# Moving the Winograd transforms of a residual block to float16 tiles and merged operations, and rescheduling its group-norm statistics

## The chip, the cores and the metric

The kernel runs on one core of one Trainium2 chip. The metric is the device time of one execution in microseconds (us), the median over the runs that are quoted. The kernel before takes 567.0 us in six runs.

The engines are named as in the profile: PE (TensorE matmuls), PEld (TensorE weight loads), DVE (VectorE), ACT (ScalarE), POOL (GpSimd) and SP (SyncE, which issues most DMAs). A line such as L628 is a line of the kernel file.

## The reference

The function is one residual block of a diffusion network, with B = 2 samples, C = 512 channels, 64 x 64 pixels and an embedding of E = 1152, all in bfloat16.

```python
def reference(x, t_emb, g1, be1, w1, w_emb, g2, be2, w2):
    def gn(z, gamma, beta): ...        # group norm, 4 groups, eps 1e-5
    def conv3(z, w): ...               # 3x3 convolution, padding 1, 512 -> 512 channels
    h = conv3(silu(gn(x, g1, be1)), w1)
    h = h + (silu(t_emb) @ w_emb).reshape(B, C, 1, 1)
    h = conv3(silu(gn(h, g2, be2)), w2)
    return x + h
```

## The kernel before

Each convolution is a Winograd transform F(4,3) along the rows: four output rows are made from six "positions" of six input rows. The work is cut into 32 **sets**. A set is one layer (of 2), one chunk of 32 image rows (4 chunks: two samples of two chunks) and one tile of 128 output channels (`ot`, 4 of them). A set has 6 positions x 4 input channel tiles (`ct`) x 3 column taps = 72 matmuls of 128x128 weights on 128x512 data, so the 32 sets have 2304. I number the sets 1 to 32. Sets 1 to 16 are the first convolution (`layer == 0`), sets 17 to 32 the second.

Four kinds of work surround the matmuls:

- **U**, the transformed weights. For each of the 32 pairs (`ot`, `ct`) of the two layers, TensorE transposes nine 128x128 blocks into PSUM, ScalarE copies them out and VectorE forms the four mixed positions.
- **V**, the transformed input of a chunk. ScalarE applies group norm and SiLU to one channel tile, VectorE forms six positions from it. A chunk has four such parts, and the first set of a chunk (sets 5, 9, 13 ...) can't finish before all four are there.
- **The output transform** (`evac`): six PSUM banks of a set become four output rows.
- **Group-norm statistics.** Those of the second layer (`gn2`) end in a tiny matmul whose result stands in one of two shared PSUM banks (`ps_x`). The weight transposes of U go through the same two banks.

All but the matmuls is cut into steps that a small scheduler, `_Background`, hands out after each position of a set, earliest deadline first. A deadline is a slot number; a set has six slots.

The parts that the change touches (cuts marked with `...`):

```python
KAPPA = 1.0 / 6.0
...
def gn2_task(b, stats):                    # four output tiles, one step each
    for ot in range(CT):
        gn2_finalize(b, ot, *stats[ot])    # sums -> tiny matmul into ps_x -> scale and bias
        yield
...
def prep_U(layer, ot, ct, eng=None, dep=None):
    ...                                    # DMA of the weights, 9 transposes into pa, pb (ps_x)
    nc.scalar.copy(out=U[:, :, 0:NPOS:NPOS - 1, :], in_=pa[:])
    nc.scalar.copy(out=g1t[:], in_=pb[:])
    yield                                                    # sb_, U, g1t are BF16, cc is F32
    nc.vector.tensor_tensor(out=sb_[:], in0=g0, in1=g2, op=ALU.add)
    nc.vector.tensor_tensor(out=U[:, :, 1, :], in0=sb_[:], in1=g1t[:], op=ALU.add)
    nc.vector.tensor_tensor(out=U[:, :, 2, :], in0=sb_[:], in1=g1t[:], op=ALU.subtract)
    yield
    nc.vector.scalar_tensor_tensor(out=cc[:], in0=g0, scalar=0.25, in1=g2, op0=ALU.mult, op1=ALU.add)
    nc.vector.scalar_tensor_tensor(out=U[:, :, 3, :], in0=g1t[:], scalar=0.5, in1=cc[:], ...)
    nc.vector.scalar_tensor_tensor(out=U[:, :, 4, :], in0=g1t[:], scalar=-0.5, in1=cc[:], ...)
    yield
...
def produce_V(...):                        # one part; all tiles BF16
    nc.scalar.activation(out=at[...], in_=ap, func=ACT.Silu, bias=..., scale=...)
    yield
    nc.vector.tensor_scalar(out=vqf, in0=rows2(1), scalar1=4.0, ...)     # first chunk: on ScalarE
    nc.vector.tensor_tensor(out=vqf, in0=vqf, in1=rows2(3), op=ALU.subtract)
    nc.vector.tensor_tensor(out=Vc[:, 1], in0=p_, in1=q, op=ALU.add)
    nc.vector.tensor_tensor(out=Vc[:, 2], in0=p_, in1=q, op=ALU.subtract)
    nc.vector.tensor_tensor(out=vsf, in0=rows2(3), in1=rows2(1), op=ALU.subtract)
    nc.vector.tensor_scalar(out=s2, in0=s_, scalar1=2.0, ...)            # first chunk: on ScalarE
    nc.vector.tensor_tensor(out=Vc[:, 3], in0=r_, in1=s2, op=ALU.add)
    ...                                    # seven more: 5 tensor_tensor and 2 tensor_scalar of 528 columns
...
def evac(pos):                             # all temporaries F32
    if pos == 1:   nc.scalar.activation(out=c1[:], in_=accs[1][:], func=ACT.Copy, scale=KAPPA)
    elif pos == 2: # t1 = KAPPA*acc2 + c1 ; c1 = 2*c1 - t1           (2 scalar_tensor_tensor)
    elif pos == 3: nc.scalar.activation(out=c3[:], in_=accs[3][:], func=ACT.Copy, scale=KAPPA)
    elif pos == 4: # t2 = KAPPA*acc4 + c3 ; c3 = 2*c3 - t2 ; rows 1 and 2, tt, ss
                   # layer 0: 6 operations; layer 1: 10, with the residual rows
    elif pos == 0: # row 0 = acc0 + tt
    elif pos == 5: # row 3 = acc5 + ss, then the output DMA
...
for layer in range(2):
    for idx, (b, ch) in enumerate(chunks):
        for ot in range(CT):
            ...                            # one set: 6 x (12 matmuls, one scheduler tick, evac)
        if layer == 0 and ch == NCH - 1:   # sums of a sample complete: statistics of layer 2
            bg.finish(t_emb_task)
            t_gn2[b] = bg.add(gn2_task(b, ...), CT, slot_of(0, idx, CT - 1) + SLOTS + 2 * SLOTS)
```

Of the kernel before, what the change touches and what calls it, by code (L numbers as in the profile page):

```python
# [10 lines left out]
ALU = mybir.AluOpType  # L11
AX = mybir.AxisListType
F32 = mybir.dt.float32
BF16 = mybir.dt.bfloat16
PSUM = bass.MemoryType.PSUM
# [48 lines left out]
def kernel(  # L64
# [22 lines left out]
    NKX = 3  # L87
# [8 lines left out]
    KAPPA = 1.0 / 6.0  # L96
    FAST_U = "s"
    ACT_TS0 = True
    N_SUM_ACT = 1
    RES_ON_PE = False  # L100
# [20 lines left out]
    h_scr = dpool.tile([B, CT, P, HW], BF16, name="h_scr")  # L121
# [13 lines left out]
    a_tmp = [consts.tile([P, CR + 4, WP], BF16, name=f"a_tmp{i}") for i in range(2)]  # L135
    for at in a_tmp:
        nc.gpsimd.memset(at[:, :, 0:WP:WP - 1], 0.0)
    vq = consts.tile([P, TR, 2, WP], BF16, name="vq")
    vs = consts.tile([P, TR, 2, WP], BF16, name="vs")
    vq2 = consts.tile([P, TR, 2, WP], BF16, name="vq2")  # L140
    vt = consts.tile([P, 2, 3, TR, WP], BF16, name="vt")
# [119 lines left out]
    def gn2_finalize(b, ot, ssum, ssq):  # L261
        m0 = small.tile([P, 2], F32, name="m0")
        nc.vector.reduce_sum(out=m0[:, 0:1], in_=ssum[:], axis=AX.X)
# [24 lines left out]
    def prep_U(layer, ot, ct, eng=None, dep=None):  # L288
        wn = stage.tile([P, CQ], BF16, tag="stage")
        after((eng or nc.sync).dma_start(out=wn[:], in_=w_v[layer][ot][:, ct * CQ:(ct + 1) * CQ]),  # L290
              dep() if dep else None)
        U = upool.tile([P, NKX, NPOS, P], BF16, tag="U")
        Ut[layer][ot][ct] = U
        wn_v = wn[:].rearrange("p (c ky kx) -> p kx ky c", ky=3, kx=3)
        yield
        pa = ps_x.tile([P, NKX, 2, P], BF16, tag="x")
        for kx in range(NKX):
            for j in range(2):
                nc.tensor.transpose(pa[:, kx, j, :], wn_v[:, kx, 2 * j, :], ident[:])  # L299
        pb = ps_x.tile([P, NKX, P], BF16, tag="x")  # L300
        for kx in range(NKX):
            nc.tensor.transpose(pb[:, kx, :], wn_v[:, kx, 1, :], ident[:])
        nc.scalar.copy(out=U[:, :, 0:NPOS:NPOS - 1, :], in_=pa[:])  # L303
        g1t = wtmp.tile([P, NKX, P], BF16, tag="g1t")
        nc.scalar.copy(out=g1t[:], in_=pb[:])  # L305
        g0 = U[:, :, 0, :]
        g2 = U[:, :, NPOS - 1, :]
        if FAST_U == "both":
            g0q = wtmp.tile([P, NKX, P], BF16, tag="g0q")
            nc.scalar.activation(out=g0q[:], in_=pa[:, :, 0, :], func=ACT.Copy, scale=0.25)  # L310
            g1h = wtmp.tile([P, NKX, P], BF16, tag="g1h")
            nc.scalar.activation(out=g1h[:], in_=pb[:], func=ACT.Copy, scale=0.5)
            yield
            sb_ = wtmp.tile([P, NKX, P], BF16, tag="sb")
            nc.vector.tensor_tensor(out=sb_[:], in0=g0, in1=g2, op=ALU.add)
            nc.vector.tensor_tensor(out=U[:, :, 1, :], in0=sb_[:], in1=g1t[:], op=ALU.add)
            nc.vector.tensor_tensor(out=U[:, :, 2, :], in0=sb_[:], in1=g1t[:], op=ALU.subtract)
            yield
            cb_ = wtmp.tile([P, NKX, P], BF16, tag="sb")
            nc.vector.tensor_tensor(out=cb_[:], in0=g0q[:], in1=g2, op=ALU.add)  # L320
            nc.vector.tensor_tensor(out=U[:, :, 3, :], in0=cb_[:], in1=g1h[:], op=ALU.add)
            nc.vector.tensor_tensor(out=U[:, :, 4, :], in0=cb_[:], in1=g1h[:], op=ALU.subtract)
            yield
            return
        if FAST_U == "s":
            yield
            sb_ = wtmp.tile([P, NKX, P], BF16, tag="sb")
            nc.vector.tensor_tensor(out=sb_[:], in0=g0, in1=g2, op=ALU.add)
            nc.vector.tensor_tensor(out=U[:, :, 1, :], in0=sb_[:], in1=g1t[:], op=ALU.add)  # L329
            nc.vector.tensor_tensor(out=U[:, :, 2, :], in0=sb_[:], in1=g1t[:], op=ALU.subtract)  # L330
            yield
            cc = wtmp.tile([P, NKX, P], F32, tag="sc")
            nc.vector.scalar_tensor_tensor(out=cc[:], in0=g0, scalar=0.25, in1=g2, op0=ALU.mult, op1=ALU.add)  # L333
            nc.vector.scalar_tensor_tensor(out=U[:, :, 3, :], in0=g1t[:], scalar=0.5, in1=cc[:],  # L334
                                           op0=ALU.mult, op1=ALU.add)
            nc.vector.scalar_tensor_tensor(out=U[:, :, 4, :], in0=g1t[:], scalar=-0.5, in1=cc[:],  # L336
                                           op0=ALU.mult, op1=ALU.add)
            yield
            return
        yield  # L340
        sc = wtmp.tile([P, NKX, P], F32, tag="sc")
        nc.vector.tensor_tensor(out=sc[:], in0=g0, in1=g2, op=ALU.add)
        nc.vector.tensor_tensor(out=U[:, :, 1, :], in0=sc[:], in1=g1t[:], op=ALU.add)
        nc.vector.tensor_tensor(out=U[:, :, 2, :], in0=sc[:], in1=g1t[:], op=ALU.subtract)
        yield
        cc = wtmp.tile([P, NKX, P], F32, tag="sc")
        nc.vector.scalar_tensor_tensor(out=cc[:], in0=g0, scalar=0.25, in1=g2, op0=ALU.mult, op1=ALU.add)
        nc.vector.scalar_tensor_tensor(out=U[:, :, 3, :], in0=g1t[:], scalar=0.5, in1=cc[:],
                                       op0=ALU.mult, op1=ALU.add)
        nc.vector.scalar_tensor_tensor(out=U[:, :, 4, :], in0=g1t[:], scalar=-0.5, in1=cc[:],  # L350
                                       op0=ALU.mult, op1=ALU.add)
        yield
# [29 lines left out]
    POS_ORDER = (1, 2, 3, 4, 0, 5)  # L382
    Vt = {}
    V_STEPS = 3 * CT

    def produce_V(layer, b, ch, resident=None, V=None, act_ts=False):
        if V is None:
            V = vpool.tile([P, CT, NPOS, TR, WP], BF16, tag="V")
# [3 lines left out]
        vqf = vq[:].rearrange("p t f w -> p t (f w)")  # L392
        vsf = vs[:].rearrange("p t f w -> p t (f w)")
        for ct in range(CT):
# [5 lines left out]
            if resident is None:  # L400
                src = srcp.tile([P, CR + 2, W], BF16, tag="src")
# [12 lines left out]
            for (a_, b_, ap) in srcs:  # L414
                nc.scalar.activation(  # L415
# [3 lines left out]
                )  # L419
            if not act_ts:  # L420
                yield

            def rows(j):
                return at[:, j:j + TH * (TR - 1) + 1:TH, :]
# [3 lines left out]

            Vc = V[:, ct]
            if act_ts:  # L430
                vqx = (vq, vq2)[ct % 2]
                vqxf = vqx[:].rearrange("p t f w -> p t (f w)")
                s2, r4, s4 = (vt[:, ct % 2, i] for i in range(3))
                nc.scalar.activation(out=vqxf, in_=rows2(1), func=ACT.Copy, scale=4.0)
                yield
                nc.vector.tensor_tensor(out=vqxf, in0=vqxf, in1=rows2(3), op=ALU.subtract)
# [127 lines left out]
# [3 lines that stand above are left out]
# [16 lines left out]
                if layer == 0 and idx == 1 and ot == 0:  # L583
                    t_emb_task = bg.add(emb_task(), EMB_STEPS, slot_of(0, 1, CT - 1))
# [178 lines left out]
```

## Time and profile before

| | kernel before |
|---|---|
| median of the 16 runs that stand beside the changed kernel's | 567.76 us |
| range | 566.2 to 568.52 us |
| span of the profiled run | 566.0 us |
| TensorE / VectorE / ScalarE busy | 542.5 / 480.2 / 218.5 us |
| mean step from one main matmul to the next, undisturbed | 0.218 us |

These are the head of the profile page of the kernel before, and its table of 40 slices of the span, in which each digit is the busy share of a slice in tenths.

```profile
span 566.0 us, 7697 instructions
PE 542.5 (96%) x2812; PEld 260.6 (46%) x2814; DVE 480.2 (85%) x1226; ACT 218.5 (39%) x252; POOL 23.1 (4%) x74
...
PE   5879999899999999999999989999999999999995
...
DVE  2889999989988884898879999999999997555665
ACT  5699999363335332343236204322130300000000
```

TensorE is busy nearly all the time. VectorE is close to it, with 85%, but that average hides stages: it is busy for 90% or more in slices 4 to 8 (about 42 to 113 us) and again around the layer boundary (slices 22 to 33, about 300 to 465 us), and about half idle at the end.

The chain of work that ended last says what the span is made of. The first line is its share by engine, the second one stretch of it (start, us, what).

```profile
PE 73%; DVE 20%; issue 2%; DMA 2%; POOL 1%; ACT 1%; SPq 0%; DVEq 0%; ACTq 0%
...
348.07 206.73 PE acc L628 x948
```

From 348 to 555 us the chain is one unbroken run of main matmuls; the output transform of the last set follows on it. 206.73 us for 948 of them is 0.218 us each, so 2304 need 502 us at that pace (an estimate). The first main matmul starts at 26.1 us and the output follows the last one by some 6 us. What can be won lies in the start, in the tail and in the places where TensorE stops.

Where it stops, the list of TensorE's waits shows (what waits <- whom it waits for: us in total, times, longest). Left out are the first 30 us with the wait for the first input (6.3 us) and those for the first statistics, and waits of 0.7 us or less:

```profile
PE acc L628 <- DVE V L448: 3.1, 2, 1.9
PE pa L299 <- DVE tot L165: 2.3, 1, 2.3
PE acc L628 <- DVE V L457: 1.6, 1, 1.6
PE acc L628 <- ACT c L635: 0.9, 1, 0.9
```

The first is the start: V parts of the first chunk. The third and fourth lie at 107 and 113 us. The second is at the layer boundary. The timeline of TensorE shows those (start, us, engine, line, what, count, and in brackets the idle time ahead and its releaser):

```profile
99.83 6.93 PE L628 MATMUL acc<-V,U 128*128 128x512 bf16 x31
...
108.38 5.13 PE L628 MATMUL acc<-V,U 128*128 128x512 bf16 x22 [1.62 <-DVE V L457]
...
114.44 0.60 PE L628 MATMUL acc<-V,U 128*128 128x512 bf16 x2 [0.93 <-ACT c L635]
...
338.78 0.80 PE L299 MATMUL pa<-ident,wn 128*128 128x128 bf16 x6 [2.34 <-DVE tot L165]
```

At 106.8 us the second chunk's V isn't ready. At 336.4 us a weight transpose needs a shared bank in which a statistics result waits for VectorE to copy it out (`tot`), and VectorE is busy with its queue. The next view counts busy time in three stretches of 2 us around that wait. Its columns are the stretch and its length, the busy time of PE, PEld, DVE, ACT and POOL with counts, the granted TensorE clock, the DMA share and GB/s.

```profile
336.00:338.00 2.00, 0.44 (x3) 0.14 (x1) 2.00 (x5) 0.00 (x0) 0.00 (x0) 1.00 0.00 0
338.00:340.00 2.00, 1.22 (x10) 1.06 (x10) 1.77 (x8) 0.38 (x1) 0.65 (x2) 0.66 0.10 16
340.00:342.00 2.00, 2.00 (x10) 1.06 (x9) 1.66 (x9) 1.30 (x3) 0.82 (x3) 0.50 0.80 289
```

VectorE is busy for the whole of 336 to 338 us, and TensorE stands from 336.4 us on. Then the clock is granted at only half speed until 342 us, and the wait costs more than its 2.34 us: the trace holds a dip of 3.41 us at 0.5, in which main matmuls come 0.43 us apart (four from 339.69 us) in place of 0.218. That is at most 1.7 us of lost work (an estimate: half of 3.41).

Three groups of VectorE operations show the prices that the change is about (line, engine, operation, out<-in with sizes and type, count | busy us, mean ns | idle before):

```profile
L654 DVE SCALAR_TENSOR_TENSOR t<-acc,c 128x512 f32<-128x512 f32 x32 | 22.0, 686 | 31.3 <-PE acc L628 31.3
...
L455 DVE TENSOR_TENSOR vq<-vq,a_tmp 128x1056 bf16<-128x1056 bf16 x28 | 19.7, 702 | 0.1
...
L333 DVE SCALAR_TENSOR_TENSOR cc<-U 128x384 f32<-128x384 bf16 x32 | 17.6, 551 | 0.0
```

A tensor_tensor on 1056 bf16 columns (702 ns) costs about as much as a scalar_tensor_tensor on 512 fp32 columns (686 ns).

### The profile page before, as it was taken

How to read it: one execution, taken by the hardware profiler on the slowest of the kernel's cores; microseconds unless marked ns; L12 is line 12 of the kernel's file. 1: busy time of each engine (PE TensorE's matmuls, PEld its weight loads, DVE VectorE, ACT ScalarE, POOL GpSimd, SP SyncE). 2: the span in 40 equal slices, each digit the busy share in tenths (PEclk: the TensorE clock that was granted, in tenths of full speed). 3: DMA queues.
4: the chain of work that ended last, by engine and by line, in shares of the span. 5: the costliest groups of instructions: out<-in, count | busy, mean ns of one | idle time of the engine just before them, and what ended most of it. 6: DMA issues, size and time to landing. Idle time of an engine off the chain costs nothing.

```text
span 566.0 us, 7697 instructions
## 1 busy us (share of the span) xinstructions
PE 542.5 (96%) x2812; PEld 260.6 (46%) x2814; DVE 480.2 (85%) x1226; ACT 218.5 (39%) x252; POOL 23.1 (4%) x74
## 2 busy tenths in 40 slices
PE   5879999899999999999999989999999999999995
PEld 4535544344444444444445545444444444444442
DVE  2889999989988884898879999999999997555665
ACT  5699999363335332343236204322130300000000
POOL 1110000011001100000000010000000000000000
PEclk9999999999999999999999999999999999999999
DMA  8506554333523120132123502323433022222210
GB/s 334 208 22 230 184 179 135 131 125 128 146 75 115 65 88 37 58 130 83 41 97 101 175 22 76 112 97 128 151 93 100 36 75 74 75 74 76 74 39 37
DMA packets 18754, 59.83 MB, mean 106 GB/s; under 512 B 2075, under 2 KB 3227, under 8 KB 18331
## 3 DMA queue, kind: packets, MB, share of 16 engines
q1 hardware_dynamic: 18656, 59.32, 30.9%
q8 instruction: 22, 0.36, 0.3%
q14 instruction: 17, 0.14, 0.1%
q10 hardware_dynamic: 59, 0.01, 0.0%
HBM read 42.54 MB, written 16.78 MB: 105 GB/s over the span
## 4 chain that ended last, share of the span: by engine, by line
PE 73%; DVE 20%; issue 2%; DMA 2%; POOL 1%; ACT 1%; SPq 0%; DVEq 0%; ACTq 0%
PE acc L628 70%; DVE U L336 2%; DVE U L334 1%; PE pa L299 1%; DVE U L329 1%; PE gr L199 1%; DMA xbuf<-in_x_dram 1%; DVE U L330 1%; POOL rstd L178 1%; DVE cc L333 1%; DMA wn<-in_w_dram 1%; DVE t L642 1%; DVE vq L455 1%; DVE t L654 1%; DVE yst L662 1%
## 5 line engine op out<-in xcount | busy, mean ns | idle before, releaser
L628 PE MATMUL acc<-V,U 128*128 128x512 bf16 x2304 | 512.0, 382 | 5.8 <-DVE V L448 3.1
L628 PEld LDWEIGHTS <-U 128*128 128x128 bf16 x2304 | 224.2, 98 | 273.7 <-issue 7.5
L415 ACT ACTIVATE a_tmp<-src,nb_all,sc_all 128x2112 bf16<-128x2112 bf16 x28 | 60.2, 2151 | 40.6 <-DVE V L470 26.0
L635 ACT ACTIVATE c<-acc 128x512 f32<-128x512 f32 x32 | 19.0, 593 | 118.7 <-PE acc L628 90.0
L697 ACT ACTIVATE junk<-yst 128x2048 bf16<-128x2048 bf16 x16 | 30.5, 1909 | 58.5 <-DVE yst L693 53.2
L654 DVE SCALAR_TENSOR_TENSOR t<-acc,c 128x512 f32<-128x512 f32 x32 | 22.0, 686 | 31.3 <-PE acc L628 31.3
L649 ACT ACTIVATE c<-acc 128x512 f32<-128x512 f32 x32 | 19.0, 594 | 64.5 <-PE acc L628 64.5
L303 ACT COPY U<-pa 128x768 bf16<-128x768 bf16 x32 | 25.7, 802 | 42.5 <-PE pa L299 42.5
L642 DVE SCALAR_TENSOR_TENSOR t<-acc,c 128x512 f32<-128x512 f32 x32 | 21.9, 685 | 21.9 <-issue 15.1
L656 DVE SCALAR_TENSOR_TENSOR c<-c,t 128x512 f32<-128x512 f32 x32 | 22.0, 687 | 0.4
L644 DVE SCALAR_TENSOR_TENSOR c<-c,t 128x512 f32<-128x512 f32 x32 | 22.0, 686 | 0.3
L299 PEld LDWEIGHTS <-wn 128*128 128x128 bf16 x192 | 17.1, 144 | 8.0 <-issue 3.1
L299 PE MATMUL pa<-ident,wn 128*128 128x128 bf16 x192 | 17.7, 232 | 2.4 <-DVE tot L165 2.3
L455 DVE TENSOR_TENSOR vq<-vq,a_tmp 128x1056 bf16<-128x1056 bf16 x28 | 19.7, 702 | 0.1
L459 DVE TENSOR_TENSOR vs<-a_tmp 128x1056 bf16<-128x1056 bf16 x28 | 19.6, 701 | 0.0
L336 DVE SCALAR_TENSOR_TENSOR U<-g1t,cc 128x384 bf16<-128x384 bf16 x32 | 17.7, 552 | 0.0
L334 DVE SCALAR_TENSOR_TENSOR U<-g1t,cc 128x384 bf16<-128x384 bf16 x32 | 17.6, 552 | 0.0
L333 DVE SCALAR_TENSOR_TENSOR cc<-U 128x384 f32<-128x384 bf16 x32 | 17.6, 551 | 0.0
L305 ACT COPY g1t<-pb 128x384 bf16<-128x384 bf16 x32 | 15.8, 493 | 0.0
L216 ACT ACTIVATE xt<-xt 128x2048 bf16<-128x2048 bf16 x8 | 15.4, 1928 | 0.1
L212 ACT ACTIVATE xt<-xt 128x2048 bf16<-128x2048 bf16 x8 | 15.4, 1926 | 0.0
L199 PE MATMUL gr<-xbuf 128*128 128x128 bf16 x96 | 7.9, 251 | 6.3 <-DMA xbuf<-in_x_dram 6.3
(204 smaller groups left out, 503.0 us busy)
## 6 DMA issues: line engine op xcount, KB each, us to landing
wn<-in_w_dram SPq DMA_DIRECT2D x32, 288.0 KB, 3.1
src<-h_scr SPq DMA_DIRECT2D x16, 528.0 KB, 3.7
h_scr<-yst SPq DMA_DIRECT2D x16, 512.0 KB, 2.6
xr<-in_x_dram SPq DMA_DIRECT2D x16, 512.0 KB, 4.2
out_dram<-yst SPq DMA_DIRECT2D x16, 512.0 KB, 3.5
src<-in_x_dram SPq DMA_DIRECT2D x12, 528.0 KB, 4.5
xt<-in_x_dram SPq DMA_DIRECT2D x8, 512.0 KB, 3.7
xbuf<-in_x_dram SPq DMA_DIRECT2D x3, 1024.0 KB, 6.2
```

Of the source, the lines that this page charges most:

```text
L299: nc.tensor.transpose(pa[:, kx, j, :], wn_v[:, kx, 2 * j, :], ident[:])
L303: nc.scalar.copy(out=U[:, :, 0:NPOS:NPOS - 1, :], in_=pa[:])
L333: nc.vector.scalar_tensor_tensor(out=cc[:], in0=g0, scalar=0.25, in1=g2, op0=ALU.mult, op1=ALU.add)
L334: nc.vector.scalar_tensor_tensor(out=U[:, :, 3, :], in0=g1t[:], scalar=0.5, in1=cc[:], op0=ALU.mult, op1=ALU.add)
L336: nc.vector.scalar_tensor_tensor(out=U[:, :, 4, :], in0=g1t[:], scalar=-0.5, in1=cc[:], op0=ALU.mult, op1=ALU.add)
L415: nc.scalar.activation(out=at[:, a_ - r0:b_ - r0, 1:W + 1], in_=ap, func=ACT.Silu, bias=nb_all[:, layer, b, ct:ct + 1], scale=sc_all[:, la ...
L455: nc.vector.tensor_tensor(out=vqf, in0=vqf, in1=rows2(3), op=ALU.subtract)
L628: nc.tensor.matmul(accs[pos][:], lhsT=U[ct][:, kx, pos, :], rhs=V[:, ct, pos, :, kx:kx + W], start=first, stop=last)
L642: nc.vector.scalar_tensor_tensor(out=t1[:], in0=accs[2][:], scalar=KAPPA, in1=c1[:], op0=ALU.mult, op1=ALU.add)
L644: nc.vector.scalar_tensor_tensor(out=c1[:], in0=c1[:], scalar=2.0, in1=t1[:], op0=ALU.mult, op1=ALU.subtract)
L654: nc.vector.scalar_tensor_tensor(out=t2[:], in0=accs[4][:], scalar=KAPPA, in1=c3[:], op0=ALU.mult, op1=ALU.add)
L697: nc.scalar.activation(out=junk[:], in_=yf, func=ACT.Square, scale=float(HW) ** -0.5, accum_out=ssq[:, ch:ch + 1])
```

## The change

The intent is to take work off VectorE. All transform tiles become float16 (with the weights scaled by 64, meant to keep their digits), scalar_tensor_tensor operations become pairs of 16-bit tensor_scalar and tensor_tensor operations, and two or four operations are merged into one wherever their operands lie side by side. For the output transform ScalarE now evicts four of the six banks instead of two. For V a scaled copy moves to ScalarE for every part; in the first chunk, where ScalarE had made four copies a part, it makes one. Three schedule lines move as well: the SiLU of the second chunk waits until the first eviction, the embedding task starts two sets later, and the deadline of the second sample's layer-2 statistics moves from the start of set 19 to the end of set 20. The matmuls and the transposes stay the same in number.

The diff, cut to its core (`...` marks cuts inside; the tile declarations, the deletion of branches that were never taken, and the weighting of the row sums are left out):

```diff
+F16 = mybir.dt.float16
-    KAPPA = 1.0 / 6.0
+    WS = 64.0
+    KAPPA = 1.0 / (6.0 * WS)
...                                                      # prep_U
-        nc.scalar.copy(out=U[:, :, 0:NPOS:NPOS - 1, :], in_=pa[:])
-        nc.scalar.copy(out=g1t[:], in_=pb[:])
+        nc.scalar.activation(out=U[:, 4:6], in_=pa[:], func=ACT.Copy, scale=WS)
+        gg = wtmp.tile([P, 2, NKX, P], F16, tag="gg")
+        nc.scalar.activation(out=gg[:, 1], in_=pb[:], func=ACT.Copy, scale=WS)
+        yield
-        ...                                             # 3 tensor_tensor, 3 scalar_tensor_tensor, as above
+        nc.vector.tensor_scalar(out=sc[:, 0], in0=g0, scalar1=0.25, scalar2=None, op0=ALU.mult)
+        nc.vector.tensor_scalar(out=gg[:, 0], in0=gg[:, 1], scalar1=0.5, scalar2=None, op0=ALU.mult)
+        nc.vector.tensor_tensor(out=sc[:, 1], in0=g0, in1=g2, op=ALU.add)
+        nc.vector.tensor_tensor(out=sc[:, 0], in0=sc[:, 0], in1=g2, op=ALU.add)
+        yield
+        nc.vector.tensor_tensor(out=U[:, 0:2], in0=sc[:], in1=gg[:], op=ALU.add)
+        nc.vector.tensor_tensor(out=U[:, 2:4], in0=sc[:], in1=gg[:], op=ALU.subtract)
...                                                      # produce_V
-                nc.scalar.activation(
+                after(nc.scalar.activation(
                     ... func=ACT.Silu ...
-                )
+                ), first_evac[0] if (layer, b, ch) == (0, 0, 1) else None)
-            ...                                         # the old arithmetic, and its variant for the first chunk
+            nc.scalar.activation(out=kt[:, 1, :, 1:3]..., in_=rows2(1), func=ACT.Copy, scale=4.0)
+            yield
+            nc.vector.tensor_tensor(out=kt[:, 0]..., in0=at[:, 2:CR + 2]..., in1=at[:, 0:CR]..., op=ALU.subtract)
+            nc.vector.tensor_tensor(out=pq, in0=pq, in1=rows2(3), op=ALU.subtract)
+            nc.vector.tensor_scalar(out=kt[:, 1, :, 0], in0=kt[:, 0, :, 1], scalar1=2.0, ...)
+            yield
+            nc.vector.tensor_tensor(out=Vc[:, 0:2], in0=rp, in1=sq, op=ALU.add)
+            nc.vector.tensor_tensor(out=Vc[:, 2:4], in0=rp, in1=sq, op=ALU.subtract)
+            nc.vector.tensor_scalar(out=x_tmp[:], in0=kt[:, 0, :, 0:2], scalar1=4.0, ...)
+            nc.vector.tensor_tensor(out=Vc[:, 4:6], in0=kt[:, 0, :, 2:4]..., in1=x_tmp[:]..., op=ALU.subtract)
...                                                      # the embedding task
-                if layer == 0 and idx == 1 and ot == 0:
-                    t_emb_task = bg.add(emb_task(), EMB_STEPS, slot_of(0, 1, CT - 1))
+                if layer == 0 and idx == 1 and ot == 2:
+                    t_emb_task = bg.add(emb_task(), EMB_STEPS, slot_of(0, 1, CT - 1) + SLOTS)
...                                                      # evac
+                    if pos in (1, 2, 3, 4):
+                        kw = {}
+                        if layer == 0 and pos != 2:
+                            kw["accum_out"] = acc_sum({1: 2, 3: 3, 4: 4}[pos])
+                        i_a = nc.scalar.activation(out=msl[:, SLOT[pos]], in_=accs[pos][:],
+                                                   func=ACT.Copy if not kw else ACT.Identity, scale=KAPPA, **kw)
+                    if pos == 4:
+                        nc.vector.tensor_tensor(out=sts[:, 0:2], in0=msl[:, 0:2], in1=msl[:, 2:4], op=ALU.subtract)
+                        nc.vector.tensor_tensor(out=sts[:, 2:4], in0=msl[:, 0:2], in1=msl[:, 2:4], op=ALU.add)
+                        nc.vector.tensor_tensor(out=tt[:, 0], in0=sts[:, 2], in1=sts[:, 3], op=ALU.add)
+                        nc.vector.tensor_scalar(out=qs[:, 0], in0=sts[:, 0], scalar1=8.0, ...)
+                        nc.vector.tensor_tensor(out=tt[:, 1], in0=qs[:, 0], in1=sts[:, 1], op=ALU.add)
+                        nc.vector.tensor_scalar(out=qs[:, 0], in0=sts[:, 0], scalar1=2.0, ...)
+                        nc.vector.tensor_scalar(out=qs[:, 1], in0=sts[:, 2], scalar1=4.0, ...)
+                        nc.vector.tensor_tensor(out=y4[:, 1:3] if layer == 0 else qs[:], in0=sts[:, 1:4:2], in1=qs[:], op=ALU.add)
+                        if layer == 1:
+                            ...                          # three additions of the residual rows
+                    elif pos in (0, 5):
+                        k = 0 if pos == 0 else 1
+                        nc.vector.scalar_tensor_tensor(
+                            out=y4[:, (0, 3)[k]], in0=accs[pos][:], scalar=(0.25 / WS, 1.0 / WS)[k],
+                            in1=tt[:, k], op0=ALU.mult, op1=ALU.add, **kw)
...                                                      # statistics of layer 2
                 t_gn2[b] = bg.add(gn2_task(b, [st2[(b, o)] for o in range(CT)]), CT,
-                                  slot_of(0, idx, CT - 1) + SLOTS + 2 * SLOTS)
+                                  slot_of(0, idx, CT - 1) + SLOTS + 2 * SLOTS if b < B - 1 else slot_of(1, 1, 0) - 1)
```

## The prediction

> **What bounds the kernel now.** TensorE. The page gives it 96% of the 566.0 us span, and the chain of waits puts 70% on the main matmul (L628). In undisturbed stretches of that chain, 948 main matmuls take 206.73 us, 0.218 us each, so 2304 need 502 us. Around them: the first main matmul starts at 26.1 us (timeline) and the last ends at 560.0; transposes after the start cost about 29 x 0.55 = 16 us, small statistics and embedding matmuls about 4.5. That sums to 523 of 534 us, so TensorE loses only about 11 us after its start: about 4.4 in the first set (its V tiles are late; set done at 47.3), 1.6 at 107 us (V), 0.9 at 113 (ScalarE eviction), 0.5 at 123, 2.3 at 336 (group-norm statistics hold a shared PSUM bank) and some 1.5 at the lower clock (0.91) behind that wait. The tail from the last matmul to the end is 6 us, of which 2.3 is VectorE. VectorE is 85% busy, and full from 40 to 130 and 300 to 450 us, but is rarely what TensorE waits for.
>
> **What the change does.** Matmul and transpose counts stay. By issue-to-issue steps in the trace (fp32 128x512: 0.605 us; bf16 tensor_tensor 0.345 at 528 elements, 0.62 at 1056; bf16 tensor_scalar 0.21 and 0.345):
> - Output transform: 10 (layer 1) 14 fp32 operations, 6.05 and 8.5 us a set, become float16 ones, about 4.3 and 5.6: -74 us of VectorE.
> - U: two scalar_tensor_tensor chains fewer, 2.2 to 1.83 us, x32: -12.
> - V: 4.98 to about 4.2 us, x28: -22.
> So VectorE falls from 480 to about 372 us. [...] I expect float16 to behave as bf16, on TensorE too; no run yet shows it.
> - ScalarE gains two evictions a set (0.49 us pace, plus accumulator reads in layer 0) and a scaled copy per V part (about 1 us): 218 to about 280 us. It is already full from 40 to 100 us. I count about 15 to 20 us of its queue per set there, against 16 to 18 us of TensorE; it falls behind by 3 to 6 us, which six PSUM banks (13 us of slack) absorb.
> - The second batch's layer-2 statistics move away from the layer boundary: the 2.3 us wait and its cold clock should go.
>
> **On the critical path.** Almost none of the 108 us saved on VectorE. Gains: first set about 3.2 us (ScalarE drops three copies a part, statistics come before U; set done near 44); waits and cold clock later about 5 of 6.8 us; tail about 0.9 us (shorter last chain). Sum 9 us: span about 557, time 558.
>
> **Predicted time 558 us, 80% range 553 to 565. Chances: faster by over 2% 0.28, within 2% 0.67, slower by over 2% 0.05.**
>
> **What would show it.** Right: main matmuls still 0.218 us apart in the chain; VectorE 360 to 390 us, ScalarE 270 to 295; first set done at 43 to 45.5 us; no TensorE wait at 336 us; chain on TensorE above 80%. Wrong: a longer matmul or weight load step in float16; TensorE waiting on ScalarE evictions (L579) between 40 and 120 us; float16 tensor_tensor on the strided views slower than 0.65 us per 1056 elements.
>
> **What would make it wrong.** ScalarE's full stretch stalling TensorE by more than the banks hide, or the second set's weights arriving late, costs a few us and brings it back to 562 to 567. An earlier start of the first V tile than I count would give over 2%.

The gains on the critical path came to 3.2 + 5 + 0.9 = 9.1 us, put down as 9: from a span of 566.0 us to about 557, and a time of 558. Those on VectorE came to 74 + 12 + 22 = 108 us. What the trace of the kernel before shows is 425 to 429 ns for a bf16 tensor_tensor on 528 columns, 701 to 704 on 1056, and 681 to 686 for one on 512 fp32 columns. The "13 us of slack" of the banks is an estimate: five banks of 12 matmuls at 0.218 us make 13.1.

## The result, and the profile after

| | before | after |
|---|---|---|
| median | 567.76 us (16 runs) | 559.71 us (7 runs) |
| range | 566.2 to 568.52 us | 559.53 to 560.37 us |
| span of the profiled run | 566.0 us | 558.3 us |
| TensorE busy | 542.5 us | 541.6 us |
| VectorE busy | 480.2 us | 373.7 us |
| ScalarE busy | 218.5 us | 277.5 us |

The changed kernel is correct and 1.3% faster: the ratio is 0.987, with a 95% interval of 0.9857 to 0.9882. That counts as the same time at a threshold of 2%, but the difference is well resolved.

The runs of the kernel before fall into two groups, seven at 566.2 to 566.5 us and nine at 567.7 to 568.5 us, and a wait and the clock are the likely reason (below). The changed kernel has one group.

The head and the slices of the changed kernel's page:

```profile
span 558.3 us, 7501 instructions
PE 541.6 (97%) x2811; PEld 260.3 (47%) x2814; DVE 373.7 (67%) x983; ACT 277.5 (50%) x380; POOL 22.0 (4%) x74
...
PE   4899999999999999999999999999999999999996
...
DVE  2889999388958833894659997299746942223444
ACT  5659999995856552466346332285612111111110
```

VectorE lost 106.5 us, ScalarE gained 59 us, and the span fell by 7.7 us. ScalarE is now the engine that is full from about 40 to 125 us.

The changed kernel's chain by engine, and one stretch of it:

```profile
PE 83%; DVE 6%; ACT 1%; issue 0%; POOL 0%; DVEq 0%
...
179.68 83.75 PE acc L565 x384
```

83.75 us for 384 matmuls is 0.218 us each. The float16 operands left the matmul's pace as it was. The chain on VectorE fell from 20% to 6% of the span.

Waits of TensorE in the changed kernel, with the same ones of the start left out (6.6 us for the first input, 2.1 for the first statistics, 0.6 for ScalarE):

```profile
PE pa L302 <- ACT U L306: 0.9, 2, 0.7
PE acc L565 <- DVE V L405: 0.6, 2, 0.4
PE ps L163 <- DVE tot L165: 0.5, 1, 0.5
```

The four waits shown of the kernel before came to 7.9 us; these come to 2.0. TensorE's timeline at the same places:

```profile
101.45 10.63 PE L565 MATMUL acc<-V,U 128*128 128x512 f16 x48
111.91 0.28 PE L163 MATMUL ps<-me,ones_neg 128*128 128x2 f32 x2
112.05 10.63 PE L565 MATMUL acc<-V,U 128*128 128x512 f16 x48
...
340.04 18.48 PE L565 MATMUL acc<-V,U 128*128 128x512 f16 x84
...
364.30 0.38 PE L163 MATMUL ps<-me,ones_neg 128*128 128x2 f32 x2 [0.48 <-DVE tot L165]
```

There is no stop between 101 and 122 us, and none at the layer boundary. The later statistics show up at 364 us, with a wait of 0.48 us.

The groups of operations (columns as before):

```profile
L599 DVE SCALAR_TENSOR_TENSOR yst<-acc,tt 128x512 f16<-128x512 f32 (+1 forms) x64 | 42.6, 684 | 4.1 <-PE acc L565 4.1
...
L405 DVE TENSOR_TENSOR V<-k_tmp 128x1056 f16<-128x1056 f16 x32 | 22.4, 701 | 0.0
```

The scalar_tensor_tensor that reads PSUM still costs 684 ns for 512 columns, with a float16 output. The float16 tensor_tensor on 1056 columns costs 701 ns, as the bf16 one did.

### Where the 7.7 us came from

The busy times don't tell where the time went. A table of when each set starts its last main matmul does. I worked it out from the main matmuls of both traces, counting 72 per set (us from the start of the span):

| point | before | after | after minus before |
|---|---|---|---|
| first main matmul | 26.1 | 27.6 | +1.5 |
| set 1 | 47.1 | 46.5 | -0.6 |
| set 2 | 67.7 | 67.7 | 0.0 |
| set 4 (end of chunk 1) | 100.7 | 101.1 | +0.4 |
| set 5 (first of chunk 2) | 119.7 | 117.1 | -2.6 |
| set 7 | 153.3 | 148.7 | -4.6 |
| set 8 | 169.0 | 165.3 | -3.7 |
| set 16 (end of layer 1) | 297.8 | 294.6 | -3.2 |
| set 18 | 333.7 | 330.3 | -3.4 |
| set 19 | 355.5 | 347.7 | -7.8 |
| set 20 | 371.2 | 364.8 | -6.4 |
| set 32 (last) | 559.6 | 553.2 | -6.4 |
| end of the span | 566.0 | 558.3 | -7.7 |

So the gain stands in three places: 5.0 us in sets 5 to 7, of which 0.9 comes back in set 8, where the embedding task now stands (its 36 small matmuls ran at 136.9 to 143.0 us before, in sets 6 and 7, and run at 160.5 to 165.8 us after); 4.4 us in set 19, where the statistics wait was, of which 1.4 comes back in set 20, where the statistics now stand; and 1.3 us in the tail. Another 0.7 us is lost in small steps between these (-5.0 + 0.9 - 4.4 + 1.4 - 1.3 + 0.7 = -7.7). The start gives nothing: set 1 ends 0.6 us earlier and set 2 ends at the same time.

### The profile page after: what moved, and what is told of

Same layout as the page of the kernel before. It is cut to its first block, busy times and chain, and to the rows that moved or that the text cites. A ratio compares the mean times of both kernels' runs of the same rounds, so it can differ in the third digit from the quotient of the medians.

```text
span 558.3 us, 7501 instructions
## 1 busy us (share of the span) xinstructions
PE 541.6 (97%) x2811; PEld 260.3 (47%) x2814; DVE 373.7 (67%) x983; ACT 277.5 (50%) x380; POOL 22.0 (4%) x74
## 4 chain that ended last, share of the span: by engine, by line
PE 83%; DVE 6%; ACT 1%; issue 0%; POOL 0%; DVEq 0%
PE acc L565 81%; PE pa L302 1%; DVE U L318 1%; DVE U L317 1%; PE pb L305 1%; DVE yst L599 1%; DVE sc L315 0%; DVE sts L585 0%; DVE sc L314 0%; ACT a_tmp L381 0%; ACT junk L606 0%; DVE sts L584 0%; DVE gg L313 0%; DVE sc L312 0%; PE ps L163 0%
## 5 line engine op out<-in xcount | busy, mean ns | idle before, releaser
L565 PE MATMUL acc<-V,U 128*128 128x512 f16 x2304 | 510.6, 381 | 0.8 <-DVE V L405 0.6
L565 PEld LDWEIGHTS <-U 128*128 128x128 f16 x2304 | 223.9, 98 | 268.7 <-issue 2.2
L579 ACT ACTIVATE msl<-acc 128x512 f16<-128x512 f32 x128 | 75.5, 593 | 165.8 <-PE acc L565 162.5
L584 DVE TENSOR_TENSOR sts<-msl 128x1024 f16<-128x1024 f16 x32 | 22.1, 689 | 119.9 <-ACT msl L579 119.8
L381 ACT ACTIVATE a_tmp<-src,nb_all,sc_all 128x2112 f16<-128x2112 f16 (+1 forms) x28 | 60.2, 2152 | 21.0 <-issue 8.1
L599 DVE SCALAR_TENSOR_TENSOR yst<-acc,tt 128x512 f16<-128x512 f32 (+1 forms) x64 | 42.6, 684 | 4.1 <-PE acc L565 4.1
L394 DVE TENSOR_TENSOR k_tmp<-a_tmp 128x2112 f16<-128x2112 f16 x32 | 40.1, 1252 | 3.8 <-ACT a_tmp L381 3.7
L391 ACT ACTIVATE k_tmp<-a_tmp 128x1056 f16<-128x1056 f16 x32 | 34.7, 1085 | 10.2 <-DVE V L406 10.0
L405 DVE TENSOR_TENSOR V<-k_tmp 128x1056 f16<-128x1056 f16 x32 | 22.4, 701 | 0.0
L406 DVE TENSOR_TENSOR V<-k_tmp 128x1056 f16<-128x1056 f16 x32 | 22.4, 701 | 0.0
L585 DVE TENSOR_TENSOR sts<-msl 128x1024 f16<-128x1024 f16 x32 | 21.9, 684 | 0.0
L317 DVE TENSOR_TENSOR U<-sc,gg 128x768 f16<-128x768 f16 x32 | 17.6, 552 | 0.3
L318 DVE TENSOR_TENSOR U<-sc,gg 128x768 f16<-128x768 f16 x32 | 17.6, 550 | 0.0
```

The source lines that it names most:

```text
L317: nc.vector.tensor_tensor(out=U[:, 0:2], in0=sc[:], in1=gg[:], op=ALU.add)
L318: nc.vector.tensor_tensor(out=U[:, 2:4], in0=sc[:], in1=gg[:], op=ALU.subtract)
L381: after(nc.scalar.activation(out=at[:, a_ - r0:b_ - r0, 1:W + 1], in_=ap, func=ACT.Silu, bias=nb_all[:, layer, b, ct:ct + 1], scale=sc_all ...
L391: nc.scalar.activation(out=kt[:, 1, :, 1:3].rearrange("p t f w -> p t (f w)"), in_=rows2(1), func=ACT.Copy, scale=4.0)
L394: nc.vector.tensor_tensor(out=kt[:, 0].rearrange("p t f w -> p (t f w)"), in0=at[:, 2:CR + 2].rearrange("p r w -> p (r w)"), in1=at[:, 0:C ...
L565: nc.tensor.matmul(accs[pos][:], lhsT=U[ct][:, SLOT[pos], kx, :], rhs=V[:, ct, SLOT[pos], :, kx:kx + W], start=first, stop=last)
```

## The experiments

All ratios are against the kernel before in the same rounds. Every kernel but `out_only` gave the right result. The theories are lettered anew in each expectation.

### Is float16 itself worth or costing anything?

```diff
-F16 = mybir.dt.float16
+F16 = mybir.dt.bfloat16
```

> The changed kernel with every float16 tile declared bfloat16: same instructions, same sizes. Theory A (what pays is the 16-bit width and the merged operations, not the float16 format): 559.7 us within 1 us, ratio to the kernel before 0.985 to 0.989, matmul step still 0.218 us, VectorE 374 us. Rival (float16 itself runs slower or faster on TensorE or VectorE): a shift over 2 us. Accuracy may be worse; that is not the point of the run.

Measured: 559.67 us (559.56 to 559.76), ratio 0.9863 (0.9846 to 0.988), VectorE busy 373.6 us. It is the changed kernel's time. The format does nothing for the time; float16 was meant to keep more digits, which no run measured. So the gain comes from the 16 bits (against fp32), the merging and the schedule; no run separates the first two.

### The deferral of the statistics, undone and alone

`gn2_back` undoes the deferral in the changed kernel, `gn2_alone` makes it in the kernel before.

```diff
 # gn2_back, against the changed kernel (gn2_alone is the reverse, against the kernel before)
-  slot_of(0, idx, CT - 1) + SLOTS + 2 * SLOTS if b < B - 1 else slot_of(1, 1, 0) - 1)
+  slot_of(0, idx, CT - 1) + SLOTS + 2 * SLOTS)
```

> The changed kernel with the second sample's second-layer statistics given their old, earlier deadline at the layer boundary. Theory A (moving them is what removed the stop at 336 us): the stop and its cold clock come back, plus 2.5 to 4 us, 562.2 to 563.7 us, ratio near 0.993, and TensorE waits about 2 us near the boundary. Rival B (the lighter VectorE queue would have cleared them in time anyway): under plus 1 us, no wait over 0.7 us there.

> The kernel before with only that deadline moved. Theory A: minus 2.5 to 4 us, ratio 0.993 to 0.9955, no TensorE wait at 336 us. Rival B (VectorE is so full there that the wait only moves to another operation): ratio over 0.998.

Measured medians, with the ratio against the kernel before in brackets:

| | statistics early | statistics deferred |
|---|---|---|
| all else as before | 567.76 (1) | 568.09 (1.0015, 1.0001 to 1.003) |
| all else as after | 563.26 (0.992, 0.9903 to 0.9937) | 559.71 (0.987, 0.9857 to 0.9882) |

With the lighter VectorE (and the rest of the change) the deferral is worth 3.5 us. With the heavy one it is worth nothing. These are the waits behind that, first of `gn2_back`, then of `gn2_alone`, from their lists of TensorE's waits:

```profile
PE pa L302 <- DVE tot L165: 2.8, 1, 2.8
```

```profile
PE ps L163 <- DVE tot L165: 2.5, 1, 2.5
```

In `gn2_back` the old wait is back, at 334 us. In `gn2_alone` it is no longer there, but the same kind of wait stands at 366.8 us, because VectorE is as full one set later (from 362.2 to 366.6 us, when it copies `tot` out, it has no idle time). In the set table `gn2_alone` ends set 19 at 350.6 us (4.9 us earlier than before) and set 20 at 371.9 (0.7 later): it moved the cost and won nothing. (The traced run, at 569.20 us, is 1.1 us slower than the other four; its clock stays at half for about 6.8 us at that wait, where 28 main matmuls from 367.26 us took 9.09 us; at 0.218 us each they would take 6.1.) The two parts of the change need each other here.

**The two groups of runs.** `gn2_back`, which has the old wait, has two groups too: spans of 560.1 to 560.2 at a mean granted clock of 0.998, and of 561.9 at 0.996, with one run between them (561.5 at 0.995). The kernel before has spans of 564.5 at 0.999 and about 566.1 at 0.995. The difference is 1.6 to 1.8 us each time, which is about the half of one dip of 3.41 us (1.7, the estimate from above). In the trace of the kernel before, the changes of the clock lie at 10.96 us (where its record starts), 338.64, 342.05 and, in the tail, 563.92 us: 96, 1 and 65 times 3.413 us apart. In the 3.41 us that ended where the dip began TensorE was busy for 36% of the time (1.21 us; about 31% in `gn2_back`, my counts). What decides whether a run gets the dip isn't shown. That its wait falls differently on that grid from run to run would fit the two groups, but no kernel has a trace of a run without the dip beside one with it, so it is a guess of mine. The changed kernel has neither the wait nor a second group (its clock is 0.999 or 1.0 in every run). Between the mean times of the two kernels (567.26 and 559.87) lie 7.4 us, and about 1 us of that is the dip (9 of 16 runs times 1.7 us, an estimate).

### What the start could give: the statistics of the first layer

The prediction expected 3.2 us from an earlier end of set 1, and only 0.6 came. The timeline of VectorE in the changed kernel shows why the parts of V come no sooner (start, us, what):

```profile
32.91 0.15 DVE L165 COPY tot<-ps 128x2 f32<-128x2 f32 x1
32.98 1.25 DVE L394 TENSOR_TENSOR k_tmp<-a_tmp 128x2112 f16<-128x2112 f16 x1
...
37.00 0.21 DVE L181 SCALAR_TENSOR_TENSOR nb_all<-tot,sc_all,gb 128x1 f32<-128x1 f32 x1
```

And ScalarE's timeline shows what waits for the last of these:

```profile
37.25 2.43 ACT L381 ACTIVATE a_tmp<-xh,nb_all,sc_all 128x2048 f16<-128x2048 bf16 x2 [3.37 <-DVE nb_all L181]
```

The tiny operations that finish the statistics of the last part stand in VectorE's queue between the operations of an earlier V part. ScalarE idles for 3.37 us before it can start the SiLU of that part. In the kernel before the same SiLU does wait for ScalarE's copies:

```profile
38.51 2.41 ACT L415 ACTIVATE a_tmp<-xh,nb_all,sc_all 128x2048 bf16<-128x2048 bf16 x2
```

It starts without idle time right behind three copies (36.90 to 38.51 us), 1.5 us after its statistics were done (`nb_all` ended at 37.0). So the spared copies, which the prediction counted, brought the SiLU forward by only 1.26 us: the statistics stand close behind, and they are done no earlier than before (37.2).

`stats_mid` issues the statistics of parts 1 to 3 before any V part. `stats_early` also puts the statistics of part 0 ahead of all weight transforms, and the weight transforms of parts 1 to 3 between the V parts.

```diff
 # stats_mid
+    for ct in range(1, CT):
+        stats0(ct)
     for ct in range(CT):
-        if ct + 1 < CT:
-            stats0(ct + 1)
         for _ in range(3):
             next(gen_V0)
```

> The changed kernel with the first sample's statistics of parts 1 to 3 issued before any V part. Theory C (my missed 2.7 us in the first set: statistics of the later parts stand behind long V operations in VectorE's in-order queue, so the third SiLU starts at 37.3 us): SiLU of part 3 starts before 35 us, the first set ends 2 to 4 us before 46.7 us and the kernel gains 1.5 to 4 us, ratio 0.980 to 0.985. Rival D (VectorE's total work in the first 44 us, or the weights of the second set, set the pace): the first set ends within 1 us of 46.7, or the gain is lost by 80 us; ratio 0.986 to 0.988.

```diff
 # stats_early
-    for _ in gens_U0[0]: pass
-    for _ in gens_U0[1]: pass
     stats0(0)
-    for _ in gens_U0[2]: pass
-    for _ in gens_U0[3]: pass
-    for ct in range(CT):
-        if ct + 1 < CT: stats0(ct + 1)
-        for _ in range(3): next(gen_V0)
+    for _ in gens_U0[0]: pass
+    for ct in range(1, CT): stats0(ct)
+    next(gen_V0); next(gen_V0); next(gen_V0)
+    for ct in range(1, CT):
+        for _ in gens_U0[ct]: pass
+        for _ in range(3): next(gen_V0)
```

> As the run with the statistics before the V parts, and further the statistics of part 0 before any weight transform, the weights of parts 1 to 3 after. Theory C: SiLU of part 0 starts 2 us or more before 17.6 us, the first main matmul 2 us or more before 27.6, the first set ends 3 to 6 us before 46.7; time 554 to 557.5, ratio 0.976 to 0.983. Rival D: the weights of parts 1 to 3 now hold the first set, or the second set's weights give the gain back by 80 us: within 1.5 us of 559.7.

Measured: `stats_mid` 561.11 us (0.9887, 0.9872 to 0.9902), `stats_early` 560.93 (0.989, 0.9873 to 0.9906). Both are a little slower than the changed kernel. `stats_mid` shows the mechanism clearly, and why it doesn't pay. First ScalarE's SiLU of the last part and then TensorE's timeline:

```profile
32.22 2.43 ACT L381 ACTIVATE a_tmp<-xh,nb_all,sc_all 128x2048 f16<-128x2048 bf16 x2 [1.05 <-DVE nb_all L181]
```

```profile
46.16 0.52 PE L302 MATMUL pa<-ident,wn 128*128 128x128 bf16 x6 [1.53 <-ACT U L306]
...
48.21 0.80 PE L302 MATMUL pa<-ident,wn 128*128 128x128 bf16 x6 [1.33 <-ACT U L306]
```

The SiLU starts 5.0 us earlier, and set 1 ends at 43.7 us, 2.8 earlier than in the changed kernel and inside the prediction's 43 to 45.5. But set 2 ends at 69.2, 1.5 later. TensorE comes to set 2 before its weights are there: from 43.9 to 49.1 us it only does transposes of U and waits 2.9 us for ScalarE's copies of them. The granted clock then falls to half, as the stretch of 48 to 50 us shows (columns as above, the clock is 0.50):

```profile
48.00:50.00 2.00, 1.79 (x12) 1.23 (x12) 2.00 (x8) 2.00 (x3) 0.00 (x0) 0.50 0.58 197
```

In the 3.41 us before this dip TensorE did nothing but transposes (0.8 us) and stood idle for 2.6 us, mostly in the gaps of 1.53 and 1.33 us. Before the dip at 338.6 us in the kernel before it stood idle for 2.2 us, among main matmuls (my counts). Whether the gaps brought on the dip of `stats_mid`, or the transposes had a part in it, this run doesn't separate.

`stats_early` starts the first main matmul at 25.9 us, 1.6 earlier, and ends set 1 at 47.0, later than the changed kernel: now the weight transforms stand between the V parts. What one end of the start gains the other gives back.

### Does VectorE's load count, and where?

If the load counts only where VectorE's queue is full while TensorE waits for it, idle work added early must cost time and idle work added late must not. Both kernels add scalar_tensor_tensor operations that nobody reads to the changed kernel, at position 4 of a set.

```diff
+                        if layer == 0 and idx < 2:        # pad_early: sets 1 to 8, 6 operations each
+                            for _ in range(6):
+                                nc.vector.scalar_tensor_tensor(out=qs[:, 0], in0=sts[:, 0], scalar=1.0,
+                                                               in1=sts[:, 1], op0=ALU.mult, op1=ALU.add)
 # pad_late: layer == 1 and idx >= 1 and not (idx == len(chunks) - 1 and ot == CT - 1), range(8)
```

> The changed kernel with 6 idle VectorE operations of about 0.6 us (unused results) added after the output transform of each of the first 8 sets, 3.6 us a set, 29 us in all, about what the change took off VectorE there. Theory A (of the 106 us saved on VectorE only those between about 60 and 135 us mattered, where its full queue made TensorE wait): 2 to 5 us come back, 561.7 to 564.7 us, with TensorE waits on V or evictions between 90 and 135 us. Rival (the waits there went away for another reason, such as the order of the background work): under 1 us.

> The changed kernel with 8 such operations in each of 11 sets of the second layer, 53 us of VectorE work in all, the last set left out. Theory A (VectorE is off the path there): within 0.7 us of 559.7. Rival (time follows VectorE's total): plus 2 us or more.

Measured: `pad_early` adds 28 us of VectorE busy time (401.6) and takes 565.23 us (564.26 to 565.75; 0.9962, 0.9946 to 0.9978), 5.5 more than the changed kernel and more than the 2 to 5 that I expected. It has two groups of runs as well, with spans of 562.5 to 563.0 at a clock of 0.998 and more, and of 563.9 to 564.0 below that. `pad_late` adds 56 us (430.1) and takes 559.79 (559.76 to 559.82; 0.9869, 0.9852 to 0.9885), no more than the changed kernel.

The stretch of 100 to 140 us in three kernels shows the stage that counts: the kernel before, the changed one, and `pad_early`.

```profile
100.00:140.00 40.00, 36.97 (x190) 16.98 (x189) 37.73 (x118) 17.59 (x20) 5.07 (x12) 1.00 0.35 118
```

```profile
100.00:140.00 40.00, 40.00 (x190) 18.61 (x189) 28.36 (x83) 33.93 (x40) 3.92 (x11) 1.00 0.42 137
```

```profile
100.00:140.00 40.00, 38.52 (x182) 17.55 (x180) 38.09 (x100) 31.37 (x43) 3.26 (x9) 1.00 0.42 131
```

VectorE is busy for 37.7 of 40 us before and TensorE loses 3 us. After, VectorE has 28.4 us and TensorE loses nothing, although ScalarE now has 33.9. The padding brings VectorE back to 38.1 us, and TensorE loses 1.5 us again. The waits of `pad_early` name both places, the V of chunk 2 and the embedding in set 8:

```profile
PE ps_e L339 <- ACT s_sb L329: 2.4, 1, 2.4
PE acc L565 <- DVE V L405: 2.1, 3, 1.4
```

In the set table, `pad_early` ends set 5 1.8 us later than the changed kernel, set 7 1.9 and set 8 5.7 us later, and stays there. So although VectorE is as full as before, the padding takes back only 1.9 of the 5.0 us that sets 5 to 7 had gained. The other 3.8 us come in set 8, from the wait of 2.40 us for the embedding, which the new schedule put there, and a half-clock dip of about 3.4 us that follows it (six main matmuls from 165.54 us come 0.42 us apart; at most 1.7 us, an estimate as above). The wait for `s_sb`, the SiLU of the embedding, is put down to ScalarE. In ScalarE's queue it stands behind a SiLU of V of 2.15 us, and that one had waited for VectorE's V work of the part before (`k_tmp`, 0.28 us, and 3.44 us the one before it). So there VectorE's load comes back through ScalarE.

In the late stretch the same view, first of the changed kernel and then of `pad_late`:

```profile
350.00:540.00 190.00, 189.52 (x875) 85.45 (x873) 104.13 (x236) 52.80 (x64) 4.22 (x14) 1.00 0.26 83
```

```profile
350.00:540.00 190.00, 189.51 (x874) 85.46 (x873) 156.49 (x319) 53.06 (x64) 4.22 (x14) 1.00 0.24 82
```

VectorE goes from 104 to 156 us of 190 and TensorE's busy time doesn't move by more than 0.01 us.

### Which of the three transforms gives the relief?

`out_only` keeps the new output transform and the new schedule, with the old arithmetic of U and V in 16 bits. I had left the factor 0.25 at position 0, which belongs to the new V, so its result is wrong (relative error 0.2266). Its six runs took 562.02 to 564.46 us and those of `out_only_ok`, with the same instructions, 561.91 to 563.81. `out_only_ok` mends the constant. `old_u` goes back to the old arithmetic of U alone.

```diff
 # out_only, out_only_ok and old_u: prep_U of the changed kernel
-        ...                        # 2 tensor_scalar, 2 tensor_tensor, 2 merged tensor_tensor
+        nc.vector.tensor_tensor(out=sb_[:], in0=g0, in1=g2, op=ALU.add)
+        nc.vector.tensor_tensor(out=U[:, 1], in0=sb_[:], in1=g1t, op=ALU.add)
+        nc.vector.tensor_tensor(out=U[:, 3], in0=sb_[:], in1=g1t, op=ALU.subtract)
         yield
+        nc.vector.scalar_tensor_tensor(out=cc[:], in0=g0, scalar=0.25, in1=g2, op0=ALU.mult, op1=ALU.add)
+        nc.vector.scalar_tensor_tensor(out=U[:, 0], in0=g1t, scalar=0.5, in1=cc[:], ...)
+        nc.vector.scalar_tensor_tensor(out=U[:, 2], in0=g1t, scalar=-0.5, in1=cc[:], ...)
 # out_only and out_only_ok as well: produce_V with the arithmetic of the kernel before, in F16
 # out_only_ok as well:
-  scalar=(0.25 / WS, 1.0 / WS)[k]
+  scalar=1.0 / WS
```

> The changed kernel with the old arithmetic for U and V (in 16 bits, with the old number of VectorE operations and the old scaled copies of the first chunk) and only the new output transform. VectorE should stand near 410 us, ScalarE near 250. Theory A: most of the relief between 60 and 135 us comes from the output transform; U and V give the rest, so plus 0 to 2 us, 559.5 to 561.7. Rival (U and V, which must be ready when a set starts, are what released TensorE): plus 3 us or more.

> The run with only the new output transform, with a slip of mine mended (the old V lacks a factor of 4 at position 0, which the new output transform divides out, so that run's result was wrong). Same instructions, so the same time: 561.5 to 562.8 us, and now a right result.

> The changed kernel with the old weight arithmetic alone (six operations for each weight tile, three of them at full cost), the new V and output transform kept. 12 us more on VectorE. Theory E (what released TensorE at 107 us is the shorter V chain, since it waited for V there): the fifth set ends as in the changed kernel, about 117 us, and the time stays within 1 us of 559.7. Rival F (any VectorE work in that full stretch counts alike): the fifth set ends 1 us or more later and plus 1 to 2.5 us.

Measured: `out_only` 562.13 us (0.9921, 0.9902 to 0.9939; wrong result), `out_only_ok` 563.68 (561.91 to 563.81; 0.9935, 0.9919 to 0.9951), `old_u` 562.54 (562.41 to 563.53; 0.9922, 0.9907 to 0.9938). `out_only_ok` has two groups: the profiled run at 561.91 us, with a span of 560.1 at full clock, and five at 563.6 to 563.8 us, with spans of 561.8 to 562.0 at 0.995 to 0.997. It costs 2.2 or 4 us against the changed kernel. `out_only_ok` and `old_u` both came out above what I expected of them. My theory that the output transform gives most of the early relief falls, and so does theory E of `old_u`. TensorE's largest wait between 60 and 130 us, first in `out_only_ok`, then in `old_u`:

```profile
PE ps L165 <- DVE me L226: 1.9, 1, 1.9
```

```profile
PE ps L163 <- DVE me L224: 1.3, 1, 1.3
```

| last main matmul of | before | out_only_ok | old_u | after |
|---|---|---|---|---|
| set 1 | 47.1 | 47.0 | 48.0 | 46.5 |
| set 4 | 100.7 | 101.0 | 102.1 | 101.1 |
| set 5 | 119.7 | 119.1 | 119.6 | 117.1 |
| set 7 | 153.3 | 150.8 | 151.3 | 148.7 |
| set 19 | 355.5 | 349.5 | 350.2 | 347.7 |
| set 32 | 559.6 | 555.0 | 555.6 | 553.2 |

With the new output transform alone set 5 ends at 119.1 us, only 0.6 earlier than before. With everything but the new U it ends at 119.6, though that kernel adds only 11 us of VectorE work (384.7 busy; its three scalar_tensor_tensor operations on 384 columns take 546 to 547 ns each, the tensor_tensor operations on 384 some 350). Here TensorE doesn't wait for V itself, as it did in the kernel before, but (at 107.6 and 105.3 us) for a statistics matmul of the second sample, whose operand `me` VectorE makes only at 107.1 and 104.8 us, behind the V parts of chunk 2 and an output transform. In the changed kernel `me` is there at 96.4 us. So a light output transform isn't enough, nor one with a light V: the weights count too. Of `old_u`'s 2.5 us at set 5, 1.0 was already there at set 4, from the start. Its trace has a half-clock dip at 31 us (the mean clock from 26 to 48 us is 0.92), but its runs at full clock took the same time, so the dip isn't the reason. The gain of sets 6 and 7, about 2 us, and that of the layer boundary are there with the output transform and the new schedule alone.

### Can the start be had after all?

`stats_mid` lost its gain to the weights of set 2. `u1_mid` adds to it that three of the four weight tiles of set 2 are prepared between the V parts of set 1. `u1_two` does that with two tiles and the changed kernel's order of statistics. Both also write the last output in two halves, on two DMA queues, to shorten the tail.

```diff
 # u1_mid (u1_two: range(2), and no stats0 ahead of the loop)
+    gens_U1 = [prep_U(0, 1, ct, dep=last_x0 if ct == 0 else None) for ct in range(3)]
+    for ct in range(1, CT):
+        stats0(ct)
     for ct in range(CT):
         for _ in range(3):
             next(gen_V0)
+        if ct == 0:
+            for g in gens_U1: next(g)              # the weight DMAs
+        if ct >= 1:
+            for _ in gens_U1[ct - 1]: pass
...
+                        if last_set and pos == 5:
+                            for hf, eng in ((0, nc.scalar), (1, nc.sync)):
+                                ...                # 256 of the 512 columns, and their own output DMA
```

> An attempt to beat the changed kernel: the statistics before the V parts (as in the run that gained 2.8 us in the first set and lost 4 in the second), and the second set's first three weight tiles transformed inside the first set, where TensorE has idle time; the last output tile also leaves in two halves. If the second set was late for its weights (ScalarE copies out of the transposes), its end moves from 69.2 to under 67 us and the time to 556 to 558.5, of which the tail gives 0.5 to 1. If VectorE's total work up to there sets the pace, the second set still ends at 67.5 to 69.5 us and only the tail is gained: 558.5 to 561.

> The same with the statistics where the changed kernel has them, and two weight tiles of the second set in the first. The first set ends 0 to 2 us later than 46.7, the second 0 to 2 us earlier than 67.7. Time 557 to 559.3, of which the tail gives 0.5 to 1.

Measured: `u1_mid` 559.18 us (559.14 to 559.24; 0.986, 0.984 to 0.9879), `u1_two` 559.95 (559.63 to 560.09; 0.9873, 0.9856 to 0.989). `u1_mid` ends set 2 at 66.1 us, 1.6 earlier than the changed kernel, set 4 at 99.3 and the last set at 551.9, 1.3 earlier. Both times lie above what I had expected (556 to 558.5, with set 2 under 67 us, and 557 to 559.3), in part because the tail gave nothing (the 0.5 to 1 us that I had counted for it was an estimate that no run had shown). Set 1 of `u1_mid` ends at 47.3 us, later than in `stats_mid`, so about half of the 2.8 us that `stats_mid` had in set 1 can be kept when the next set's weights come along. Its tail, from the start of the last main matmul to the end of the span, is 5.5 us against 5.2: the halves cost 0.4 us (5.53 against 5.16). In the list of DMA issues of `u1_mid` (out<-in, queue, count, KB each, and the median us from issue to landing):

```profile
out_dram<-yst SPq DMA_DIRECT2D x15, 512.0 KB, 2.8
...
out_dram<-yst SPq DMA_DIRECT2D x1, 256.0 KB, 2.9
```

This half landed no sooner than a whole one (2.9 us against 2.8), so nothing was gained from the split. It isn't a clean test of what a smaller write costs: the other half was issued 0.33 us before it, from ScalarE's queue (its landing isn't in the list), it is one transfer of the small size, and in the kernel before the 512 KB writes took 3.5 us.

`u1_mid` has the lowest median of all kernels, half a microsecond below the changed one, but in other rounds, and the two intervals overlap. No version clearly beats the changed kernel.

## Why the prediction was right

The prediction said 558 us, with 553 to 565, and the most likely outcome within 2%. Measured were 559.71 us and 1.3% faster. The sum was right for the right main reason, with one term much too large and another too small. By set 4 the start had given -0.4 us in place of 3.2, and the waits 6.8 in place of 5. These errors partly cancel, so that the sum came so close is in part luck.

- **TensorE bounds the kernel, and its pace doesn't change: right.** 0.218 us a matmul before and after.
- **VectorE 372 us and ScalarE 280 us: right.** 373.7 and 277.5 were measured.
- **Float16 behaves as bf16: right.** 701 ns for 1056 columns against 702, and `all_bf16` has the same time.
- **The wait at 336 us and its cold clock go: right, but its reason was half told.** The prediction put it down to the deferral. `gn2_alone` shows that the deferral alone only moves the wait; the lighter VectorE is needed too.
- **ScalarE's full stretch stays hidden behind the banks: right that it stays hidden.** From 100 to 140 us ScalarE is busy for 33.9 of 40 us and TensorE for all 40. That it is the banks that hide it was an estimate, which no run tests.
- **The waits later, "about 5 of 6.8 us": too small.** From set 4 to the last main matmul the gain is 6.8 us.
- **The tail, 0.9 us: near.** 1.2 was measured (6.39 to 5.16; the rounded table gives 1.3).
- **The first set, "about 3.2 us (... set done near 44)": the mis-sized term.** Set 1 ended 0.6 us earlier, at 46.5, and by set 2 nothing was left; at set 4 the changed kernel was 0.4 late. Three things were missed. The prediction counted on statistics that come before U, but nothing in the diff moves the first layer's statistics. Dropping ScalarE's copies brought the last SiLU forward by 1.26 us only, since the statistics' tiny operations behind VectorE's V work were done no earlier (37.2 us against 37.0); that the merged operations (1.25 us for one) make that queue coarser would fit, but isn't shown. And even where set 1 did end at 43.7, in `stats_mid`, set 2 waited for its weights and gave it back. The prediction had named "the second set's weights arriving late" as a danger, which is what `stats_mid` showed.
- **"Almost none of the 108 us saved on VectorE" lies on the critical path: true of the sum, too weak for one stage.** In the first eight sets 28 us put back cost 5.5 us (`pad_early`), 1.9 of it in sets 5 to 7. In the last chunks 56 us put back cost nothing (`pad_late`).

What stays open: how the 5.0 us of sets 5 to 7 divide between V, U, the output transform and the moved embedding task, since the parts don't add up one by one, neither V nor the moved embedding task was tried alone, nor was the SiLU of chunk 2 that waits for the first eviction; and whether the clock dip after `stats_mid`'s transposes is due to them or to the gaps between them.

## What to carry to other kernels

Work taken off an engine that is 85% busy but not the bottleneck isn't time won as such (here 106.5 us less gave 7.7): find the stretch where its queue is full while the bounding engine waits for something in that queue, and only the work removed there counted (28 us put back early cost 5.5, 56 us put back late nothing). Padding the suspect engine in one stretch at a time is a cheap way to find it. Two edits can need each other, as the deferral and the lighter VectorE do, so try both alone before crediting either; and a gain at the start must be followed through the next stage, which may be waiting for other inputs.
